# Cosine attention and low-rank mixer: the first batch's keys, its last pair's value products and its first mixer stage are arranged anew

## The chip, the cores and the metric

The kernel runs on one core of one Trainium2 chip. The metric is the device time of one execution in microseconds (us). The core has five engines, each with its own queue, which it works off in order: TensorE (PE in the profile, with its weight loads as PEld), VectorE (DVE), ScalarE (ACT), GpSimd (POOL) and SyncE (SP). GpSimd issues the loads of this kernel and SyncE most of the stores. Matmul results go to PSUM, which has eight banks of 512 float32 columns.

## The reference

For 8 batches, 12 heads, 448 tokens and 64 columns a head, queries and keys are normalised, their products divided by tau pass a softmax, and the values are averaged with it. The 12 heads side by side make x, 448 tokens by 768 columns. The mixer first adds a low-rank mix along the tokens (rank 32), and then a two-layer network along the columns, with 3072 hidden columns.

```
q_n = q / (norm(q) + 1e-6);  k_n = k / (norm(k) + 1e-6)
scores = q_n @ k_n.T / tau
attn = softmax(scores)
x = (attn @ v), heads side by side          # 448 x 768
u = x + (x.T @ U @ V).T                      # U: 448 x 32, V: 32 x 448
out = u + relu(u @ w_ch1) @ w_ch2            # 768 -> 3072 -> 768
```

## The kernel before, in words

**Tiles.** Heads are worked in pairs, six a batch. A token n is written as 4 s + c, with c from 0 to 3 and s from 0 to 111, so the 448 keys make four chunks of 112. `load_qk` brings the queries and keys of two or four heads, cast to bf16. `squares` and `scales` form the squares (ScalarE or VectorE, L538 and L540), their sums (L544), a logarithm and an exponential on ScalarE (L558, L559), and the inverse (L564, L566): the scale 1/(norm sqrt(tau)) of each row, kept in the tile `inv`.

**Normalised and raw keys.** `norm` multiplies queries and keys by their scales (L612, tile `xn`), transposes them on TensorE by a matmul with the identity (L468, through `flip`) and copies the result from PSUM to the tile `qkT` (L966 on ScalarE, L968 on VectorE). For the pairs listed in `RAW_KEYS` (L303: pairs 0 to 3 of batch 0) the keys aren't multiplied: they are transposed as loaded, and their scale comes in later, as the scale of the exponential, a number for each key row.

**Scores and exponentials.** `scores` forms, for a pair and a key chunk, the products of both heads into two banks (L670). A pair with normalised keys takes one exponential for both heads, 896 columns (L688). A pair with raw keys takes one for each head, 448 columns, since each head's keys have scales of their own (L683).

**Values.** `values` multiplies the exponentials by v, with a column of ones beside it which gives the softmax sum (L713): for each head four tiles t of 128 tokens, each summed over the four key chunks j. All four tiles of a head lie in one bank. All products of a head wait for all exponentials of the pair. Then VectorE takes the reciprocal of the sums (L720) and multiplies into X (L722, the array `muls` in order of heads).

**First mixer stage.** `stage0` projects X on U in three column parts, 0 to 511, 512 to 639 and 640 to 767 (L768), and copies each to A (L966, L968). For batch 0, `columns` then forms each of six column blocks of u, transposed: three matmuls of X with the identity (L744) and one of A with V (L749) add up in one bank, and one copy brings it to `uT` (L966). For the other batches u is formed by tokens (L815, L829) and transposed.

**Network.** `mlp` forms the hidden columns in 24 blocks f: six matmuls each over the column blocks of uT (L891), then relu on ScalarE or VectorE (L914, L916), then the second layer (L927) and the add of u (L938). In batch 0, the first three blocks f begin with column blocks 0 to 4, and take block 5 later.

**The order of the work** is set by a planner. Every instruction is an `Op` with an engine, an assumed duration, dependences, the buffers it takes and gives back, and a priority. TensorE's are put in streams; at each moment the planner takes the first stream (in the order in which they were made) whose next instruction is ready by its own reckoning. ScalarE's and VectorE's go by priority. PSUM banks are handed out by rings (`bank_ring`), which list the banks that a use may have and how many at a time. Before batch 0's network begins, gaps in TensorE's plan are filled with matmuls on a constant tile (L598, `warm_up`). What the planner finds becomes a fixed order on each engine; on the chip only the waits for data and buffers remain. In the kernel before, the streams of TensorE come in this order: fill, transposes, first batch's scores, values, first stage, scores of the others, network. The last part of the first stage and the last column block go in the stream of the values, and the banks of both come from `r_mm`.

Of the kernel before, what the change touches and what calls it, by code (L numbers as in the profile page):

```python
# [269 lines left out]
def kernel(  # L270
# [12 lines left out]
    nc = tc.nc  # L283

    B, H, S, D = q.shape
    C = H * D
# [15 lines left out]
    WIDE = 3  # L302
    RAW_KEYS = {(0, 0), (0, 1), (0, 2), (0, 3)}  # L303
    FILL = 0.7
# [71 lines left out]
    r_mm = bank_ring([(7,), (6,), (5,), (4,)], 3)  # L376
    r_av = bank_ring([(5,), (6,), (7,), (4,)], 2, (4, D + 8))
    r_sc = bank_ring([(0, 1), (2, 3), (4, 5)], 3)
    r_low = bank_ring([(5,), (4,), (3,), (2,), (1,), (0,)], 2)
# [29 lines left out]
    pe_tp = plan.stream("PE")  # L409
    pe_first = plan.stream("PE")  # L410
    pe_av = plan.stream("PE")
    pe_a = plan.stream("PE")
    pe_sc = plan.stream("PE")
# [241 lines left out]
    def scores(b, slots):  # L655
# [22 lines left out]
        for (p, c), sc in zip(slots, scs):  # L678
            _, _, (inv, a, scaled) = sets[p]
            attn, exps = attns[b, p]  # L680
            if (b, p) in RAW_KEYS:
                for hh in range(2):
                    exps.append(plan.add(Op("ACT", act_t(S, 0.08), lambda sc=sc, c=c, hh=hh, attn=attn, inv=inv, a=a: nc.scalar.activation(  # L683
                        out=attn.tile[0:SCH, c, hh, off:off + S], in_=sc.tile[0:SCH, hh, 0:S], func=AF.Exp,
                        scale=inv.tile[:, 1, a + hh, c:c + 1]), deps=[o, scaled], acq=[attn],
                        rel=[sc, inv], prio=0.1)))
                continue
            exps.append(plan.add(Op("ACT", act_t(2 * S, 0.08), lambda sc=sc, c=c, attn=attn: nc.scalar.activation(  # L688
                out=attn.tile[0:SCH if b < WIDE else 128, c, :, off:off + S],
                in_=sc.tile[0:SCH if b < WIDE else 128, :, 0:S], func=AF.Exp),  # L690
                deps=[o], acq=[attn], rel=[sc], prio=0.1 if b == 0 else 1)))

    def values(b, p, X):
# [9 lines left out]
        if b == 0 and p == 0:  # L703
            last_exp["first"] = [exps[0]]
        muls = []
        for hh in range(2):
            h = 2 * p + hh
            av, rd = Slot(r_av2 if BURST[b] > 2 else r_av, 1), Slot(r_rd, 1)
            for t in range(4):
                for j in range(SC):  # L710
                    first, last = t == 0 and j == 0, t == 3 and j == SC - 1
                    def fn(t=t, j=j, h=h, hh=hh, av=av):
                        nc.tensor.matmul(  # L713
                            out=av.tile[:, t, 0:D + 1],
                            lhsT=(attn if j < SC - 1 else even).tile[0:kp, j, hh, 128 * t:128 * (t + 1)],
                            rhs=v_t[b % 2][0:kp, h, j, 0:D + 1], start=(j == 0), stop=(j == SC - 1))
                    o = plan.add(Op("PE", 0.033, fn,
                        deps=exps + got[b, h, "v"] + attn_set + v_set[b] if first else (), acq=[av] if first else [],
                        rel=([attn] if even is attn else [attn, even]) if last else []), pe_av)
# [12 lines left out]
    prev = {}  # L732

    def columns(X, A, uT, muls, cc, a):

        c0 = 128 * cc
        mm = Slot(r_mm, 1)
        st = pe_a if cc < CC - 1 else pe_av
        X.uses += 1
# [3 lines left out]
        for t in range(3):  # L743
# [7 lines left out]
            start=False, stop=True, skip_group_check=True), deps=[a], rel=[A]), st)  # L751
        c = plan.add(Op("ACT/DVE", any_t(384), None, deps=[o], rel=[mm], prio=0))
        c.fn = lambda: copy_op(c, uT.tile[:, cc, 0:384], mm.tile[:, 0:384])
        return c

    def stage0(b, X, muls):
        par = b % 2
        bank = r_sc1 if b == 1 else r_low if BURST[b] > 2 else r_mm
        by_pe = b < PE_BATCHES
# [7 lines left out]
        def project(t, c0, c1, mm):  # L767
            nc.tensor.matmul(out=mm.tile[R * t:R * (t + 1), 0:c1 - c0], lhsT=U_sb[:, par, t, :],  # L768
                             rhs=X.tile[:, t, c0:c1], start=True, stop=True)

        def project_all():
            for (c0, c1), mm in zip(cols, mms):
                for t in range(4):
                    project(t, c0, c1, mm)
        if not by_pe:
            o = plan.add(Op("PE", 0.2 + 2 * pe_t(CH), project_all, deps=muls + consts[:2 + par], acq=mms + [A]), pe_a)
        for (c0, c1), mm in zip(cols, mms):
            need = [m for i, m in enumerate(muls) if i * D < c1]
            for t in range(4) if by_pe else ():
                o = plan.add(Op("PE", pe_t(c1 - c0) + 0.2 if t == 0 else 0.01,  # L780
                                lambda t=t, c0=c0, c1=c1, mm=mm: project(t, c0, c1, mm),
                    deps=need + consts[:2 + par] if t == 0 else (), acq=[mm, A] if t == 0 else [],
                    rel=[warm] if b == 0 and c0 == 0 and t == 3 else []),
                    pe_a if c1 < C else pe_av)
            a = Op("ACT/DVE", any_t(c1 - c0), None, deps=[o], rel=[mm], prio=0)
# [84 lines left out]
    def mlp(b, us, uT, ut):  # L870
# [18 lines left out]
        def up(f, mm, ccs):  # L889
            for cc in ccs:  # L890
                o = plan.add(Op("PE", pe_t(n), lambda cc=cc: nc.tensor.matmul(  # L891
                    out=mm.tile[:, 0:n], lhsT=w1_sb[:, cc, f * 128:(f + 1) * 128],
                    rhs=uT.tile[:, cc, 0:n], start=(cc == 0), stop=(cc == CC - 1)),
                    deps=([ut[cc], last_exp[0]] if b == 0 else ut if cc == 0 else []) + (
                        [w1_of[f]] if cc == 0 else []),
# [252 lines left out]
```

## Time and profile before

The median of three runs is 588.56 us (588.4 to 589.15). The profiled execution spans 586.5 us.

| what | us or share |
|---|---|
| TensorE busy | 578.0 us, 99% |
| VectorE busy | 301.7 us, 51% |
| ScalarE busy | 268.6 us, 46% |
| GpSimd busy | 89.8 us, 15% |
| first layer of the network, L891 | 233.2 us busy, 1152 matmuls |
| second layer, L927 | 231.3 us busy, 1368 matmuls |
| value products, L713 | 58.7 us busy, 1536 matmuls |
| scores, L670 | 53.3 us busy, 384 matmuls |
| exponentials, L688 and L683 | 137.8 us (161 instructions) and 17.4 us (32) |
| fill, L598 | 141 matmuls |
| chain that ended last | TensorE 94%, ScalarE 3%, VectorE 2% |

A row of a group gives the line of the kernel, the engine, the operation, the tiles, how many there are, the busy time and the mean duration of one. A row of the timeline gives the start, the time that the instructions of the row take together, and how many they are. Matmuls overlap, so their durations add up to more than the time that they take. A row of the stretches gives each engine's busy time between two moments.

### The profile page before, as it was taken

Reading aid. Unit: us, or ns where it says so; the run is one execution under the profiler, and the core shown is the slowest. Engines: PE = TensorE matmul, PEld = TensorE weight load, DVE = VectorE, ACT = ScalarE, POOL = GpSimd, SP = SyncE. Lnnn points to the kernel's source line nnn. Section 1 sums busy time; section 2 is a strip of 40 time slices with the busy share of each in tenths; the row PEclk is TensorE's granted clock in tenths of the full one; section 3 lists DMA queues with packets and bytes.
Section 4 is the critical chain, followed back from the end, with each engine's and each line's share of the span. In section 5 each row is a group of like instructions: output and inputs, shape, how many; then the busy total and the mean of one; then the engine's idle time right before and its main releaser. Section 6 shows DMA issues by size and latency. Waiting matters only on the chain.

```text
span 586.5 us, 11699 instructions
## 1 busy us (share of the span) xinstructions
PE 578.0 (99%) x4878; PEld 328.0 (56%) x4878; DVE 301.7 (51%) x725; ACT 268.6 (46%) x444; POOL 89.8 (15%) x128
## 2 busy tenths in 40 slices
PE   7999999999999999999999999999999999999997
PEld 5555656544556665555456655655446666654565
DVE  7869839999997677368514780254102241110011
ACT  7977743567443544444453445434454334024300
POOL 8234220142410050004000040000000000000000
PEclk9999999999999999999999999999999999999999
DMA  9999992799997486359355573331031100310021
GB/s 159 201 206 192 210 147 70 119 105 138 103 141 121 72 76 101 77 86 106 42 94 103 103 50 50 78 73 32 0 58 39 41 15 1 95 41 1 1 54 55
DMA packets 133332, 50.68 MB, mean 86 GB/s; under 512 B 98208, under 2 KB 133280, under 8 KB 133280
## 3 DMA queue, kind: packets, MB, share of 16 engines
q0 software_dynamic: 72160, 25.73, 38.6%
q1 hardware_dynamic: 61056, 24.19, 20.1%
q8 instruction: 38, 0.62, 0.4%
q14 instruction: 14, 0.11, 0.1%
q10 hardware_dynamic: 64, 0.02, 0.0%
HBM read 52.25 MB, written 11.01 MB: 108 GB/s over the span
## 4 chain that ended last, share of the span: by engine, by line
PE 94%; ACT 3%; DVE 2%; DMA 0%; issue 0%
PE bank L927 38%; PE bank L891 37%; PE bank L713 8%; PE bank L670 7%; ACT attn L683 2%; PE bank L815 2%; PE bank L468 1%; PE bank L768 1%; ACT sq L538 1%; DMA raw_uv<-in_q_dram 0%; DVE xn L612 0%; DVE ss L544 0%; DVE u_nat L829 0%; ACT qkT L966 0%; PE bank L749 0%
## 5 line engine op out<-in xcount | busy, mean ns | idle before, releaser
L891 PE MATMUL bank<-uT,w_sb 128*128 128x512 bf16 (+1 forms) x1152 | 233.2, 353 | 0.6 <-ACT uT L966 0.6
L927 PE MATMUL bank<-w_sb,relu 128*128 128x384 bf16 (+1 forms) x1368 | 231.3, 323 | 0.1
L688 ACT ACTIVATE attn<-bank 128x896 bf16<-128x896 f32 (+1 forms) x161 | 137.8, 922 | 112.4 <-PE bank L670 111.9
L927 PEld LDWEIGHTS <-relu 128*128 128x128 bf16 x1368 | 128.4, 98 | 90.4 <-issue 12.7
L891 PEld LDWEIGHTS <-w_sb 128*128 128x128 bf16 x1152 | 108.9, 98 | 102.9 <-issue 8.9
L914 ACT ACTIVATE relu<-bank 128x384 bf16<-128x384 f32 (+1 forms) x161 | 87.0, 541 | 142.6 <-PE bank L891 142.2
L938 DVE TENSOR_TENSOR O_sb<-bank,u_nat 128x384 f32<-128x384 f32 (+1 forms) x57 | 31.1, 548 | 184.4 <-PE bank L927 162.1
L544 DVE TENSOR_REDUCE ss<-sq 112x8 f32<-112x512 bf16 x96 | 62.6, 670 | 1.3 <-ACT sq L538 1.1
L713 PEld LDWEIGHTS <-attn 128*128 128x128 bf16 (+1 forms) x1536 | 55.7, 98 | 10.8 <-issue 3.3
L612 DVE TENSOR_TENSOR xn<-qk_nat,inv 112x512 bf16<-112x512 bf16 x91 | 58.9, 682 | 0.2
L713 PE MATMUL bank<-v_nat,attn 128*128 128x65 bf16 (+1 forms) x1536 | 58.7, 193 | 0.1
L670 PE MATMUL bank<-qkT 64*128 64x448 bf16 (+1 forms) x384 | 53.3, 357 | 1.4 <-ACT qkT L966 0.6
L490 POOL DMA_DIRECT2D qk_nat<-in_q_dram x24 | 17.5, 729 | 201.3 <-DVE xn L612 153.8
L720 DVE RECIPROCAL rd<-bank 128x4 f32<-128x4 f32 x96 | 16.7, 176 | 51.2 <-PE bank L713 50.8
L722 DVE TENSOR_TENSOR X_sb<-bank,rd 128x256 bf16<-128x256 f32 x96 | 40.1, 420 | 2.2
L540 DVE TENSOR_TENSOR sq<-qk_nat 112x512 bf16<-112x512 bf16 x89 | 34.1, 413 | 0.0
L670 PEld LDWEIGHTS <-qkT 64*128 64x128 bf16 (+1 forms) x384 | 13.2, 95 | 28.4 <-issue 24.3
L916 DVE TENSOR_SCALAR relu<-bank 128x512 bf16<-128x512 f32 (+1 forms) x31 | 19.8, 638 | 13.9 <-PE bank L891 13.7
L513 POOL DMA_DIRECT2D v_nat<-in_v_dram x30 | 22.1, 743 | 24.5 <-PE bank L713 24.5
L829 DVE TENSOR_TENSOR u_nat<-bank,X_sb 128x384 bf16<-128x384 f32 (+2 forms) x45 | 22.2, 524 | 5.4 <-PE bank L815 4.9
L490 POOL DMA_DIRECT2D qk_nat<-in_k_dram x24 | 16.8, 702 | 5.2 <-DMA w_sb<-in_moe_w_ch_dram 3.6
L683 ACT ACTIVATE attn<-bank,inv 112x448 bf16<-112x448 f32 x32 | 17.4, 654 | 0.0
(58 smaller groups left out, 182.7 us busy)
## 6 DMA issues: line engine op xcount, KB each, us to landing
qk_nat<-in_q_dram POOLq DMA_DIRECT2D x23, 224.0 KB, 5.0
qk_nat<-in_k_dram POOLq DMA_DIRECT2D x23, 224.0 KB, 5.9
w_sb<-in_moe_w_ch_dram POOLq DMA_DIRECT2D x4, 1152.0 KB, 21.3
w_sb<-in_moe_w_ch_dram POOLq DMA_DIRECT2D x8, 576.0 KB, 16.0
v_nat<-in_v_dram POOLq DMA_DIRECT2D x17, 168.0 KB, 8.9
out_dram<-O_sb SPq DMA_DIRECT2D x15, 168.0 KB, 2.2
out_dram<-O_sb SPq DMA_DIRECT2D x16, 144.0 KB, 2.1
out_dram<-O_sb SPq DMA_DIRECT2D x16, 120.0 KB, 2.0
```

The source lines that it names most:

```text
L490: ops = [load(lambda i=i, src=src: nc.gpsimd.dma_start(out=ld.tile[:, i, lo:lo + h1 - h0, :], in_=src[b, h0:h1].rearrange("h (s c) d -> s ...
L540: nc.vector.tensor_mul(y, x, x)
L544: lambda i=i, a0=a0, a1=a1, sq=sq: nc.vector.reduce_sum(ss.tile[:, i, a0:a1, :].rearrange("p h c -> p (h c)"), sq.tile[:, 0:a1 - a0, :].re ...
L612: nc.vector.tensor_mul(dst, src, sc)
L670: nc.tensor.matmul(out=out, lhsT=qkT.tile.rearrange("p b s -> p (b s)")[r, n0:n0 + w], rhs=qkT.tile[r, SC:2 * SC, :].rearrange("p c s -> p ...
L688: exps.append(plan.add(Op("ACT", act_t(2 * S, 0.08), lambda sc=sc, c=c, attn=attn: nc.scalar.activation(out=attn.tile[0:SCH if b < WIDE el ...
L713: nc.tensor.matmul(out=av.tile[:, t, 0:D + 1], lhsT=(attn if j < SC - 1 else even).tile[0:kp, j, hh, 128 * t:128 * (t + 1)], rhs=v_t[b % 2 ...
L722: muls.append(plan.add(Op("DVE", dve_t(256), lambda av=av, rd=rd, h=h: nc.vector.tensor_mul(X.tile[:, :, h * D:(h + 1) * D], av.tile[:, :, ...
L891: o = plan.add(Op("PE", pe_t(n), lambda cc=cc: nc.tensor.matmul(out=mm.tile[:, 0:n], lhsT=w1_sb[:, cc, f * 128:(f + 1) * 128], rhs=uT.tile ...
L914: nc.scalar.activation(out=relu.tile[:, f, 0:n], in_=mm.tile[:, 0:n], func=AF.Relu)
L927: nc.tensor.matmul(out=mm.tile[:, 0:c1 - c0], lhsT=relu.tile[:, f, i * 128:(i + 1) * 128], rhs=w2_t[:, f, c0:c1], start=(f == 0), stop=(f ...
L938: nc.vector.tensor_add(out=O.tile[:, 0:w], in0=mm.tile[:, 0:w], in1=us[i].tile[:, c0:c1]),
```

## The change

All of it concerns batch 0, in the first 42 us of the run. It has four parts.

1. `RAW_KEYS` holds pairs 0 and 1 alone. The keys of pairs 2 and 3 are normalised, and their exponentials take both heads at once. The planner's assumed duration of a 448-column exponential rises (0.08 becomes 0.143 in its fixed part).
2. In pair 5, the last of batch 0, the value products go by key chunk: those of chunk j, of both heads, depend on the exponentials of chunk j alone. The sums of the four token tiles of a head are thus open at once in one bank, and the start flag is set only on the first matmul of the bank. The products of batch 0 have bank rings of their own (`r_av0`, and `r_av5` for the last pair).
3. In batch 0, each of the three projections and each column block of the first stage gets a stream by its part: `pe_z0` for parts that need only the first heads, `pe_z1` for block 4, `pe_z2` for block 5, the last two ahead of the values. Their banks come from a ring over all eight (`r_z`). A projection is one `Op` of four matmuls that stay together, where before other work could come between.
4. The copy of the last column block to uT is split in halves of 192 columns, one on ScalarE and one on VectorE, with a priority ahead of the others.

Its purpose is to shorten the way from the first loads to the first network matmuls. The core of the diff:

```diff
-    RAW_KEYS = {(0, 0), (0, 1), (0, 2), (0, 3)}
+    RAW_KEYS = {(0, 0), (0, 1)}
...
+    r_av0 = bank_ring([(5,), (6,)], 2, (4, D + 8))
+    r_av5 = bank_ring([(5,), (6,), (0,), (1,), (2,), (3,)], 2, (4, D + 8))
+    r_z = bank_ring([(7,), (4,), (6,), (5,), (3,), (1,), (2,), (0,)], 4)
...
     pe_first = plan.stream("PE")
+    pe_z2 = plan.stream("PE")
+    pe_z1 = plan.stream("PE")
     pe_av = plan.stream("PE")
+    pe_z0 = plan.stream("PE")
     pe_a = plan.stream("PE")
...
-                    exps.append(plan.add(Op("ACT", act_t(S, 0.08), lambda sc=sc, c=c, hh=hh, attn=attn, inv=inv, a=a: nc.scalar.activation(
+                    exps.append(plan.add(Op("ACT", act_t(S, 0.143), lambda sc=sc, c=c, hh=hh, attn=attn, inv=inv, a=a: nc.scalar.activation(
...
+        ends = b == 0 and p == NPAIR - 1
+        ready = attn_set + v_set[b]
+        if ends:
+            for j in range(SC):
+                for hh, (av, rd) in enumerate(list(heads)):
+                    h = 2 * p + hh
+
+                    def fn(h=h, hh=hh, j=j, av=av):
+                        for t in range(4):
+                            product(h, hh, t, j, av, j == 0 and t == 0)
+                    o = plan.add(Op("PE", 4 * 0.033, fn, deps=[exps[j]] + got[b, h, "v"] + ready,
+                                    acq=[av] if j == 0 else [], rel=[attn] if j == SC - 1 else []), pe_av)
...
+    pe_z = [pe_z0] * (CC - 2) + [pe_z1, pe_z2]
...
-        mm = Slot(r_mm, 1)
-        st = pe_a if cc < CC - 1 else pe_av
+        mm = Slot(r_z, 1)
+        st = pe_z[cc]
...
-        c = plan.add(Op("ACT/DVE", any_t(384), None, deps=[o], rel=[mm], prio=0))
-        c.fn = lambda: copy_op(c, uT.tile[:, cc, 0:384], mm.tile[:, 0:384])
-        return c
+        cs = []
+        mm.uses = mm.left = 1 if cc < CC - 1 else 2
+        for n in range(mm.uses):
+            e, r = ("ACT/DVE", slice(0, 384)) if cc < CC - 1 else (("ACT", "DVE")[n], slice(192 * n, 192 * n + 192))
+            c = plan.add(Op(e, any_t(384 // mm.uses), None, deps=[o], rel=[mm], prio=0 if cc < CC - 1 else -1))
+            c.fn = lambda c=c, r=r: copy_op(c, uT.tile[:, cc, r], mm.tile[:, r])
+            cs.append(c)
+        return cs
...
-        bank = r_sc1 if b == 1 else r_low if BURST[b] > 2 else r_mm
+        bank = r_z if b == 0 else r_sc1 if b == 1 else r_low if BURST[b] > 2 else r_mm
...
+            if by_pe:
+                o = plan.add(Op("PE", 0.2 + pe_t(c1 - c0), lambda c0=c0, c1=c1, mm=mm: project_part(c0, c1, mm),
+                                deps=need + consts[:2 + par], acq=[mm, A],
+                                rel=[warm] if b == 0 and c0 == 0 else []),
+                             pe_z[c0 // 128] if b == 0 else pe_a if c1 < C else pe_av)
```

## The prediction

> **What bounds the kernel now.** I read the busy shares and the slices first, then the waits of TensorE, then the first 42 us engine by engine.
>
> ```profile
> PE 578.0 (99%) x4878; PEld 328.0 (56%) x4878; DVE 301.7 (51%) x725; ACT 268.6 (46%) x444; POOL 89.8 (15%) x128
> PE   7999999999999999999999999999999999999997
> ACT  7977743567443544444453445434454334024300
> ```
>
> TensorE is busy from end to end, so only work taken off it, or an earlier start of its real work, can shorten the run. The waits of TensorE after 41.8 us fill one line, and even that wait ends at 41.80:
>
> ```profile
> PE bank L891 <- ACT uT L966: 0.6, 1, 0.6
> ```
>
> So from 41.8 us TensorE runs a fixed amount of work without waiting. Before that, part of its busy time is filler (L598), and ScalarE is what is full:
>
> ```profile
> core 0: us, PE busy (x) PEld busy (x) DVE busy (x) ACT busy (x) POOL busy (x), PEclk, DMA share, GB/s
> 8.00:20.00 12.00, 10.15 (x127) 6.26 (x126) 10.80 (x26) 11.94 (x27) 6.63 (x9) 1.00 1.76 188
> 20.00:36.50 16.50, 15.87 (x222) 9.03 (x221) 11.60 (x36) 16.02 (x28) 5.32 (x7) 1.00 1.21 208
> 36.50:41.80 5.30, 4.71 (x65) 2.84 (x63) 4.61 (x13) 2.76 (x8) 2.16 (x3) 1.00 1.26 207
> 41.80:75.00 33.20, 33.20 (x318) 20.08 (x318) 28.22 (x67) 23.37 (x42) 10.50 (x14) 1.00 1.37 201
> ```
>
> The reader is to see 27.96 of 28.5 us of ScalarE busy from 8 to 36.5, and then a stretch of 5.3 us in which no engine but TensorE is full. Two rows of ScalarE's timeline give the price of its work:
>
> ```profile
> 21.57 8.48 ACT L683 ACTIVATE attn<-bank,inv 112x448 bf16<-112x448 f32 x16
> 29.83 6.67 ACT L688 ACTIVATE attn<-bank 112x896 bf16<-112x896 f32 x8
> ```
>
> The exponentials of a pair with raw keys are eight of 448 columns, since each head needs its own scale; those of other pairs are four of 896. From 21.57 to 29.83 are 16 of the first: 0.516 us each. Of the second, (6.67 - 0.92) / 7 = 0.821 us. A pair costs 4.13 or 3.28 us. After the last exponential (36.50) comes a chain that TensorE can't fill:
>
> ```profile
> 36.34 1.31 PE L713 MATMUL bank<-v_nat,attn 112*128 112x65 bf16 x32
> 37.94 0.42 DVE L722 TENSOR_TENSOR X_sb<-bank,rd 128x256 bf16<-128x256 f32 x1
> 38.75 0.33 PE L891 MATMUL bank<-uT,w_sb 128*128 128x384 bf16 x1
> 39.35 0.49 PE L891 MATMUL bank<-uT,w_sb 128*128 128x384 bf16 x2
> 40.20 0.23 PE L768 MATMUL bank<-X_sb,U_sb 128*32 128x128 bf16 x3
> 40.55 0.33 PE L891 MATMUL bank<-uT,w_sb 128*128 128x384 bf16 x1
> 40.90 0.34 PE L749 MATMUL bank<-V_sb,A_sb 128*128 128x384 bf16 x1
> ```
>
> In these 5.3 us only four first-layer matmuls (L891) get in.
>
> [...] Half as many instructions must save. [...] here 22 matmuls of L891 in 3.73 us are 0.163 us apart though their rows say 326 ns, so I count with distances. [...]
>
> **The change, part by part.**
>
> 1. *Keys of pairs 2 and 3 normalised.* ScalarE loses 2 x (4.13 - 3.28) = 1.7 us. VectorE gains two products of 0.60 us (L612: two in 1.27), 1.2 us. TensorE loses eight small transposes; nothing, since filler stands beside them. Added waiting: the scores of pair 2 now need its keys too. I follow VectorE in the new order. Its second reduction for heads 4 to 7 waits for a square on ScalarE that ends at 14.25, and ends at 14.97; the roots are on ScalarE till about 15.75, the inverse till 16.4, one more reduction to 17.0, two products to 18.25, a third to 18.85, two copies to 19.5. Scores then start near 20.0, behind pair 0's products, which need v (TensorE's first L713 is at 19.12). ScalarE gets there after eight exponentials of pair 1 and two squares, at 20.45, so the wait lies between 0 and 0.3. Pair 3 is ready at 22.2 and wanted at 24.1, pair 4 at 26.8 and 27.8, pair 5 at 28.8 and 31.1: VectorE stays ahead by 1 us or more.
>
> ScalarE's sum from 13.17, where both kernels have had the same sequence: before, 3 copies of 0.41, 3 squares of 0.52, 2 pairs of roots of 0.40, 24 x 0.516, 8 x 0.821, which is 22.5 and would end at 35.8 with the last one's tail of 0.1; it ended at 36.50, so 0.7 were waits. After: 2 copies, 4 squares, the same roots, 8 x 0.516 and 16 x 0.821, which is 21.0, ending at 34.2. With 0.3 for waits: last exponential at 34.55, 1.95 earlier. With none 34.25; with the old 0.7, 34.95.
>
> 2. *Last pair's products by key tile.* 32 products stood after the last exponential (36.34 to 37.65). Now 24 stand beside the exponentials and 8 are left: 8 x 0.033 + 0.16 for the last one's end, from 34.65 to 35.07. Both heads end together, so VectorE then does reciprocal, reciprocal, product, one column copy (it stands between in the new order) and product: 0.2 + 0.2 + 0.34 + 0.47 + 0.42 = 1.63, to 36.78. Before, the second head's product ended at 38.36, 1.86 after the last exponential; now 2.23. On this step alone nothing is won: the copy costs what the tile order saves.
>
> 3. *First stage by parts, streams and banks.* The gain is here: before, the last projection (L768) was pulled apart at 39.77 and 40.20 behind other parts, 1.84 us after its X was there, and its A copy stood behind two reductions on VectorE (40.55), so L749 came at 40.90 and uT at 41.75. After: projection at 36.88, three identity matmuls with it (0.35, as 39.00 to 39.35 before), four L891 matmuls (0.65) which hide the A copy on ScalarE (0.31), the last V product at 37.88, and from 38.05 a run of 39 first-layer matmuls. Nine of these need only the other columns: 9 x 0.163 = 1.47 us, which hide the last column's two half copies, even one after the other (0.3 each). By 38.05 six first-layer matmuls are done, before 41.80 four.
>
> Four of the five early columns (L744, L749) and the copies to uT lie on TensorE and ScalarE from 35.0 to 37.0, beside step 2's chain on VectorE: nothing. The half copy's wait on VectorE, with squares of the next batch ahead and normalisations behind it, costs nothing while those 1.47 us last. The planner's corrected price for L683 changes no instruction.
>
> *Sum.* 41.80 - 38.05 = 3.75, plus two more matmuls done, 0.33: 4.1 us. After it both orders hold the same matmuls of each shape, so 588.56 - 4.1 = **584.5**.
>
> Can the rest take it? Weights: the last chunk of the second layer is issued at 53.25 and takes 22.3 us, so it lands at 75.5; it is wanted after 63 second-layer matmuls that begin near 68, with others between near 83. The next-but-one batch's queries and keys land at 76.7 and 77.9 (56.33 + 20.4, 58.86 + 19.0) and VectorE reaches them near 82. Neither binds.
>
> **The rivals.**
>
> - *VectorE becomes the bound in the attention.* For: it is busy 11.60 of 16.5 and 10.80 of 12 us. Against: the margins of step 1. If the norms delayed ScalarE by all that it saves, the last exponential would stay near 36.5 and only steps 2 and 3 remain: 4.1 - 1.95, 2.1 us, 586.4.
> - *Gain given back at the next seam.* The second batch's transposes now stand behind 39 first-layer matmuls and begin near 44.4, before 45.38: one us earlier, where the first layer begins four earlier. Its last uT copy ended at 107.34, 1.76 us ahead of its first use at 109.10; by distances that use is now near 104.2, and the copy would end near 104.0. If it keeps only the 1 us, it ends at 106.3: TensorE waits 2.2 us, 586.7. Against: part of its chain was itself waiting for TensorE's turn.
> - *Slower.* VectorE is in order; a late load of the next-but-one batch ahead of the second batch's adds would stop it. It takes more than 5 us margin + 4 us gain: landing near 88 instead of 78 gives some 589.8. Only an upset DMA queue would do that, and the loads keep their order.
>
> **How the numbers follow.** Forecast 0.68, VectorE 0.13, seam 0.11, slower 0.05, no change 0.03. The low end takes no waits (0.3 better) and both columns' slack, 583.8; the high end takes the first two rivals in, 587.0. Faster: 0.68 + 0.13 + 0.11 and thus 0.92, which I cut to 0.89, for what an order with so many new places may hide; same 0.04, slower 0.07.
>
> **What would show it.** Right: last exponential at 34.3 to 35.0; 16 exponentials of 448 and 8 more of 896 than before; the long first-layer run from about 38; no TensorE wait over 0.5 us after it. Wrong: ScalarE idle before pair 2 or 4 and released by TensorE's scores; TensorE waiting for uT near 104 or for w_sb near 70 to 83.

## The result and the profile after

The changed kernel took 585.65 us in the median of four runs (585.09 to 586.07), the kernel before 588.86 in four runs beside it (588.4 to 589.32). The ratio is 0.9945, with a 95% interval of 0.9928 to 0.9962. A second measurement gave 585.84 against 588.53, ratio 0.9956 (0.9943 to 0.9968). So the change saves about 3 us, 3.2 in the first pair of medians and 2.7 in the second, where 4.1 were forecast. Lines of the code have moved: score matmuls are L676 (before L670), the exponentials L689 and L694 (L683, L688), the value products L717 (L713), their division L745 and L747 (L720, L722), projections L800 (L768), the columns' identity and V matmuls L771 and L776 (L744, L749), the copies L1001 and L1003 (L966, L968), the first layer L926 (L891), filler L604 (L598).

The profile shows one execution of each kernel. That of the changed kernel took 586.07 us, the longest of its four, and that of the kernel before 588.53; its spans therefore differ by 2.3 us (586.5 and 584.2) and not by 3.2. The page of the changed kernel, busy shares and slices:

```profile
PE 573.4 (98%) x4851; PEld 327.8 (56%) x4871; DVE 304.4 (52%) x731; ACT 265.8 (46%) x433; POOL 89.6 (15%) x128
ACT  7976643377623536343443455434454334024300
```

As before, only TensorE is full. A slice is 14.6 us long, and in the first three, where the change lies, ScalarE's digits are those of before; the slices are too coarse to show it. The stretches that the prediction had cut, in the changed kernel (columns: window, length, busy time of each engine with its instructions, granted clock, DMA share, GB/s):

```profile
20.00:36.50 16.50, 15.11 (x259) 10.31 (x258) 13.46 (x42) 15.24 (x22) 5.99 (x7) 1.00 1.21 208
36.50:41.80 5.30, 5.30 (x46) 3.30 (x44) 5.12 (x13) 2.91 (x8) 2.16 (x3) 1.00 1.27 206
```

From 36.5 to 41.8 TensorE is now busy for 5.30 of 5.30 us (before 4.71), and the work is real: the hole after the last exponential has closed. VectorE pays for it from 20 to 36.5: 13.46 us instead of 11.60. ScalarE's exponentials, two rows of its timeline:

```profile
16.22 3.77 ACT L689 ACTIVATE attn<-bank,inv 112x448 bf16<-112x448 f32 x7
28.70 6.71 ACT L694 ACTIVATE attn<-bank 112x896 bf16<-112x896 f32 x8
```

The last exponential ends at 28.70 + 6.71 = 35.41 (before 36.50). There are 16 of 448 columns and 16 of 896, where before there were 32 and 8. What TensorE does behind it:

```profile
28.95 1.02 PE L717 MATMUL bank<-v_nat,attn 112*128 112x65 bf16 x27
...
35.64 0.24 PE L800 MATMUL bank<-X_sb,U_sb 128*32 128x128 bf16 x4
35.82 0.34 PE L771 MATMUL bank<-ident,X_sb 128*128 128x128 bf16 x3
35.99 0.41 PE L717 MATMUL bank<-v_nat,attn 112*128 112x65 bf16 x8
...
38.14 0.24 PE L800 MATMUL bank<-X_sb,U_sb 128*32 128x128 bf16 x4
...
38.49 0.81 PE L926 MATMUL bank<-uT,w_sb 128*128 128x384 bf16 x4
39.14 0.33 PE L776 MATMUL bank<-V_sb,A_sb 128*128 128x384 bf16 x1
39.30 6.50 PE L926 MATMUL bank<-uT,w_sb 128*128 128x384 bf16 x39
```

The shape is the one that was forecast: last eight products, projection, four first-layer matmuls, last V product, and the run of 39. It begins at 39.30 (forecast 38.05), with six first-layer matmuls done ahead of it, as forecast. Before, with four done, it began at 41.80:

```profile
41.80 3.73 PE L891 MATMUL bank<-uT,w_sb 128*128 128x384 bf16 x22 [0.57 <-ACT uT L966]
```

Below, *tail* is the distance from the end of the last exponential to the start of the long first-layer run. Since kernels have different numbers of first-layer matmuls behind them by then, tails are also given "at four done": 0.163 us, the distance of two first-layer matmuls in these traces (39 of them take 6.50 us in the changed kernel, one alone 0.33), is taken off for each matmul above four and added for each below. Before: 5.30. Changed kernel: 3.89, and 3.89 - 2 x 0.163 = 3.56 at four done. Times from the start of the span are to be compared with care: the first exponential comes at 8.55 to 8.78 us in ten of the fourteen profiles, and at 9.23 or 9.34 in the other four, both profiles of the changed kernel among them.

### The profile page after: what moved, and what is told of

The parts are those of the page before. It is cut to its first block, busy times and chain, and to the rows that moved or that the text cites. A ratio compares the mean times of both kernels' runs of the same rounds, so it can differ in the third digit from the quotient of the medians.

```text
span 584.2 us, 11649 instructions
## 1 busy us (share of the span) xinstructions
PE 573.4 (98%) x4851; PEld 327.8 (56%) x4871; DVE 304.4 (52%) x731; ACT 265.8 (46%) x433; POOL 89.6 (15%) x128
## 4 chain that ended last, share of the span: by engine, by line
PE 94%; DVE 3%; ACT 1%; DMA 1%; issue 0%; DVEq 0%
PE bank L962 38%; PE bank L926 37%; PE bank L717 8%; PE bank L676 7%; PE bank L850 2%; PE bank L474 1%; DVE xn L618 1%; DVE ss L550 1%; PE bank L800 1%; ACT attn L689 1%; DMA raw_uv<-in_q_dram 1%; ACT sq L544 0%; DVE qkT L1003 0%; PE bank L771 0%; PE bank L896 0%
## 5 line engine op out<-in xcount | busy, mean ns | idle before, releaser
L926 PE MATMUL bank<-uT,w_sb 128*128 128x384 bf16 (+1 forms) x1133 | 228.8, 352 | 1.2 <-issue 0.3
L694 ACT ACTIVATE attn<-bank 128x896 bf16<-128x896 f32 (+1 forms) x169 | 144.0, 917 | 114.6 <-PE bank L676 114.5
L926 PEld LDWEIGHTS <-w_sb 128*128 128x128 bf16 x1152 | 109.5, 98 | 102.7 <-issue 7.2
L717 PEld LDWEIGHTS <-attn 128*128 128x128 bf16 (+1 forms) x1536 | 55.6, 98 | 9.5 <-issue 3.3
L618 DVE TENSOR_TENSOR xn<-qk_nat,inv 112x512 bf16<-112x512 bf16 x93 | 60.5, 682 | 0.2
L717 PE MATMUL bank<-v_nat,attn 128*128 128x65 bf16 (+1 forms) x1536 | 58.7, 193 | 0.3 <-DVE X_sb L747 0.2
L676 PE MATMUL bank<-qkT 64*128 64x448 bf16 (+1 forms) x384 | 51.1, 357 | 1.3 <-ACT attn L689 0.8
L745 DVE RECIPROCAL rd<-bank 128x4 f32<-128x4 f32 x96 | 16.9, 178 | 48.7 <-PE bank L717 48.4
L747 DVE TENSOR_TENSOR X_sb<-bank,rd 128x256 bf16<-128x256 f32 x96 | 40.0, 419 | 2.1
L676 PEld LDWEIGHTS <-qkT 64*128 64x128 bf16 (+1 forms) x384 | 13.0, 95 | 29.1 <-issue 25.2
L850 PE MATMUL bank<-A_sb,V_sb 128*128 128x384 bf16 (+2 forms) x62 | 14.4, 312 | 0.2 <-issue 0.2
```

The costliest lines, as they stand in the source:

```text
L618: nc.vector.tensor_mul(dst, src, sc)
L676: nc.tensor.matmul(out=out, lhsT=qkT.tile.rearrange("p b s -> p (b s)")[r, n0:n0 + w], rhs=qkT.tile[r, SC:2 * SC, :].rearrange("p c s -> p ...
L717: nc.tensor.matmul(out=av.tile[:, t, 0:D + 1], lhsT=(attn if j < SC - 1 else even).tile[0:kp, j, hh, 128 * t:128 * (t + 1)], rhs=v_t[b % 2 ...
L747: muls.append(plan.add(Op("DVE", dve_t(256), lambda av=av, rd=rd, h=h: nc.vector.tensor_mul(X.tile[:, :, h * D:(h + 1) * D], av.tile[:, :, ...
```

## The experiments

Of the kernels below, those of one group ran on one chip beside the kernel before. They are read by two numbers: the ratio of times, with its interval, and the tail in the profile.

### First group: which part brings how much

**The last two pairs' keys raw again, all else as in the changed kernel.**

```
-    RAW_KEYS = {(0, 0), (0, 1)}
+    RAW_KEYS = {(0, 0), (0, 1), (0, 2), (0, 3)}
```

> The changed kernel with the keys of four pairs raw again, as before; all else of the change stays. My theory (part 1 shortens ScalarE's exponentials by 1.95 us and the rest comes from the first stage): the last exponential ends about 1.7 to 2 us later than in the changed kernel, and the time is 1.5 to 2 us above it, some 587.4. Rival (VectorE's added products eat part of the gain by delaying the value path): under 1 us above the changed kernel, some 586.4. Rival (the keys are all of the gain): back at 588.9.

Measured: 587.01 us, ratio 0.9969 (0.9958 to 0.998). The last exponential ends at 36.89, no earlier than before. The tail is 3.04 us, 2.88 at four done: shorter than the changed kernel's. On TensorE, and on ScalarE:

```profile
32.70 0.28 PE L604 MATMUL bank<-warm 128*128 128x128 bf16 x2
...
39.93 1.30 PE L926 MATMUL bank<-uT,w_sb 128*128 128x384 bf16 x7
```

```profile
35.58 0.49 ACT L1001 CAST uT<-bank 128x384 bf16<-128x384 f32 x1
35.94 0.95 ACT L694 ACTIVATE attn<-bank 112x896 bf16<-112x896 f32 x1
```

TensorE still has room for filler at 32.70, as before (32.85). In the changed kernel the last filler stands at 27.36: from 28.95 on it works without a pause to the end of the attention. So parts 2 and 3 alone shorten the tail by 5.30 - 2.88 = 2.4 us, where I had forecast 2.1 for them. Some of this is only moved: a column copy of 0.49 us stands ahead of the last exponential here, where before all such copies came behind it. So a second count is needed, from the first exponential to the run, at four done: 33.13 us before, 30.54 here, 31.40 with part 1 alone (the next kernel), 29.74 in the changed kernel. By it parts 2 and 3 gain 2.6, part 1 gains 1.7, and both together 3.4 (3.6 in the second profile of the changed kernel). So 0.7 to 0.9 us of the sum is lost when part 1 is added. The times can't resolve so little: by the ratios it is 1.8 and 1.7 us alone against 2.6 to 3.2 together, each uncertain by 0.6 to 1.0.

**Part 1 alone on the kernel before**, with the planner's price for the exponential of 448 columns.

```
-    RAW_KEYS = {(0, 0), (0, 1), (0, 2), (0, 3)}
+    RAW_KEYS = {(0, 0), (0, 1)}
...
-                    exps.append(plan.add(Op("ACT", act_t(S, 0.08), lambda sc=sc, c=c, hh=hh, attn=attn, inv=inv, a=a: nc.scalar.activation(
+                    exps.append(plan.add(Op("ACT", act_t(S, 0.143), lambda sc=sc, c=c, hh=hh, attn=attn, inv=inv, a=a: nc.scalar.activation(
```

> The kernel before with the keys of two pairs raw and the new assumed cost of the 448-column exponential; nothing else of the change. My theory: the last exponential ends 1.7 to 2 us earlier than before, the time falls by 1.5 to 2 us to about 587.0. Rival (VectorE's products eat it): 588.0 or more. Rival (the keys are all of the gain): 585.7.

Measured: 586.85 us, ratio 0.9971 (0.9961 to 0.9981). Its ScalarE and its TensorE (the lines are those of the kernel before):

```profile
27.95 6.71 ACT L688 ACTIVATE attn<-bank 112x896 bf16<-112x896 f32 x8
```

```profile
39.97 3.73 PE L891 MATMUL bank<-uT,w_sb 128*128 128x384 bf16 x22 [0.57 <-ACT uT L966]
```

The exponentials end at 34.66, 1.84 us earlier, and the tail is 39.97 - 34.66 = 5.31, the old one to 0.01 us. The 1.84 us come through to the end: the median is 2.24 us below that of the kernel before (1.7 by the ratio). By these numbers part 1 does what step 1 says. The planner's new price is in this kernel too; what it does in the changed kernel is the last of these experiments.

**The changed kernel without the order by key tile.**

```
-        ends = b == 0 and p == NPAIR - 1
+        ends = False
```

> The changed kernel with the last pair's value products by token tile again, all of them after the pair's last exponential. My theory (tile order alone wins nothing, since both heads then end together and a column copy stands between): within 0.3 us of the changed kernel, 585.4 to 586.0. Rival (24 products of 0.032 us fewer behind the last exponential are on the path): 0.8 us slower, 586.4.

Measured: 585.95 us, ratio 0.9957 (0.9944 to 0.9969). Exponentials end at 34.51, the run begins at 38.17 with three matmuls done: a tail of 3.66, 3.82 at four done, 0.26 longer than with the order by key tile. The time can't be told from the changed kernel's.

**The changed kernel with the first stage in the old streams and banks**; its projection stays one operation.

```
-        mm = Slot(r_z, 1)
-        st = pe_z[cc]
+        mm = Slot(r_mm, 1)
+        st = pe_a if cc < CC - 1 else pe_av
...
-        bank = r_z if b == 0 else r_sc1 if b == 1 else r_low if BURST[b] > 2 else r_mm
+        bank = r_sc1 if b == 1 else r_low if BURST[b] > 2 else r_mm
...
-                              pe_z[c0 // 128] if b == 0 else pe_a if c1 < C else pe_av)
+                              pe_a if c1 < C else pe_av)
```

> The changed kernel with the first stage of the first batch in the streams and from the banks of before; each projection still one operation, the last copy still in halves. My theory (the first stage's own streams give about 2 us): about 2 us slower than the changed kernel, 587.6. Rival (the projection as one operation and the tile order gave that already): 586 or less.

Measured: 586.1 us, ratio 0.9953 (0.9939 to 0.9966). The profiled execution is the longest of five (588.05): it waited 0.8 us for a load of v, and its granted clock was 0.50 from 19.3 to 26.1 us. Both lie ahead of the last exponential, so only its tail is used: 41.24 - 36.92 = 4.32, with four done. That is 0.76 longer than the changed kernel's 3.56, and 0.98 shorter than before. I had put the whole gain of step 3 on streams and banks; a good half of it is there without them. The time does not even show the 0.76. One thing is better here than in the changed kernel:

```profile
37.18 0.41 PE L717 MATMUL bank<-v_nat,attn 112*128 112x65 bf16 x8
```

The last eight products begin 0.26 us after the last exponential, and in the changed kernel 35.99 - 35.41 = 0.58.

### Second group: step 3 taken apart

**The changed kernel again**, to stand beside the others.

> The changed kernel unchanged, on the chip of the runs beside it: the yardstick for them, and a second profile. It tells whether the late first exponential (9.23 us in the first profile of the changed kernel, 8.67 before) and the wait of 0.4 us near 87 us belong to the kernel. Theory: the start varies from execution to execution, so here the first exponential may be near 8.6 and the last near 34.6; the wait near 87 us stands. Rival: the start is late again. Time 585.6 to 585.9 on both.

Measured: 585.84 us, ratio 0.9956 (0.9943 to 0.9968); exponentials end at 35.17, the run begins at 39.07, six done: tail 3.90, as in the first profile (3.89). The first exponential is late again (9.23), so my theory of the start failed and its rival came true; the wait of 0.4 us near 87 us stands, as expected.

**Part 1 and only the streams and banks.**

```
+    r_z = bank_ring([(7,), (4,), (6,), (5,), (3,), (1,), (2,), (0,)], 4)
...
+    pe_z = [pe_z0] * (CC - 2) + [pe_z1, pe_z2]
...
-        mm = Slot(r_mm, 1)
-        st = pe_a if cc < CC - 1 else pe_av
+        mm = Slot(r_z, 1)
+        st = pe_z[cc]
...
-        bank = r_sc1 if b == 1 else r_low if BURST[b] > 2 else r_mm
+        bank = r_z if b == 0 else r_sc1 if b == 1 else r_low if BURST[b] > 2 else r_mm
...
-                    pe_a if c1 < C else pe_av)
+                    pe_z[c0 // 128] if b == 0 else pe_a if c1 < C else pe_av)
```

> The kernel before with part 1 and with the first stage's own streams and banks; its projections still four single operations, the value products by token tile, the last copy whole. Theory (streams and banks are what shortens the chain after the last exponential): the chain from the last exponential to the long first-layer run shrinks from 5.3 to about 4 us, time 1 us under part 1 alone, about 585.8, and the same as the changed kernel. Rival (tile order, single projection and half copies each carry a share): 586.4.

Measured: 586.19 us, ratio 0.996 (0.9947 to 0.9972). Exponentials end at 34.73, the run begins at 38.63 with three done: tail 3.90, 4.06 at four done. Against part 1 alone (5.31) the streams and banks bring 1.25 us.

**Part 1 and only the projection as one operation.**

```
-            for t in range(4) if by_pe else ():
-                o = plan.add(Op("PE", pe_t(c1 - c0) + 0.2 if t == 0 else 0.01,
...
+            if by_pe:
+                o = plan.add(Op("PE", 0.2 + pe_t(c1 - c0), lambda c0=c0, c1=c1, mm=mm: project_part(c0, c1, mm),
```

> The kernel before with part 1 and with each projection as one operation of four matmuls; streams, banks, products and copies as before. Theory (the split of the projection at the end was only a consequence of its stream): within 0.3 us of part 1 alone, about 586.7. Rival (keeping the four together is what freed the chain): 586.0 or less.

Measured: 586.64 us, ratio 0.9968 (0.9955 to 0.998). Tail 39.60 - 34.77 = 4.83, four done: 0.48 us less than part 1 alone. The two together would make 5.31 - 1.25 - 0.48 = 3.58 at four done if they added up, and the whole changed kernel has 3.56, with the order by key tile in it. So they overlap with the 0.26 of that order; all are of one chain. All this is read from tails: the times of this kernel, of the one before it and of part 1 alone can't be told apart.

**The last column copied whole by one engine.**

```
-        mm.uses = mm.left = 1 if cc < CC - 1 else 2
+        mm.uses = mm.left = 1
...
-            e, r = ("ACT/DVE", slice(0, 384)) if cc < CC - 1 else (("ACT", "DVE")[n], slice(192 * n, 192 * n + 192))
+            e, r = ("ACT/DVE", slice(0, 384))
```

> The changed kernel with the last column block copied whole, on one engine. Theory (the copy is hidden behind nine first-layer matmuls, 1.47 us): within 0.2 us of the changed kernel. Rival (the half copies are on the path): 0.3 us slower.

Measured: 585.86 us, ratio 0.9954 (0.994 to 0.9968); tail 38.38 - 34.49 = 3.89, six done, 3.56 at four. The halves bring nothing, as step 3 said: what they feed stands behind other first-layer matmuls.

### Third group: does more of the same help, and where is it given back?

**One raw pair instead of two.**

```
-    RAW_KEYS = {(0, 0), (0, 1)}
+    RAW_KEYS = {(0, 0)}
```

> The changed kernel with the keys of pair 1 normalised as well; only pair 0's stay raw. If ScalarE's exponentials were still the bound, the last one would end 4.13 - 3.28 = 0.85 us earlier and the time fall to about 585.0. Theory after the runs so far: VectorE has no slack left there, since two more of its products (0.6 us each) stand ahead of pair 1's scores; ScalarE waits for scores, and the time is not under the changed kernel's, 585.7 or more.

Measured: 593.71 us, ratio 1.0086 (1.0072 to 1.01): slower. The exponentials end at 35.68 and the run begins at 39.48 with six done: 0.2 us behind the changed kernel, so the loss of 8 us is not there. ScalarE does lose what fewer exponentials were to save: from the first (8.63) to the last they take 27.05 us, in the changed kernel 26.18. It waits 0.9 us for transposes and 0.5 us for scores, as the theory had it, and makes four of the copies to qkT instead of two. The large loss is later. Four windows of this kernel (columns as before):

```profile
104.00:108.00 4.00, 2.88 (x47) 1.69 (x44) 3.45 (x14) 2.21 (x4) 0.00 (x0) 1.00 0.10 29
108.00:112.00 4.00, 0.60 (x5) 0.40 (x5) 3.99 (x9) 1.40 (x2) 1.39 (x2) 0.83 0.53 88
112.00:116.00 4.00, 3.81 (x41) 2.52 (x41) 3.54 (x13) 2.07 (x4) 0.00 (x0) 0.50 1.39 140
116.00:120.00 4.00, 4.00 (x18) 1.43 (x17) 2.92 (x8) 1.79 (x3) 0.00 (x0) 0.82 0.54 83
```

From 108 to 112 TensorE (the first busy column) works 0.60 us of 4 while VectorE (the third) works 3.99, and the granted clock falls, to 0.50 in the next window. The longest wait of TensorE, and what VectorE does meanwhile:

```profile
112.19 1.42 PE L676 MATMUL bank<-qkT 64*128 64x448 bf16 x4 [2.41 <-DVE u_nat L861]
```

```profile
107.28 2.50 DVE L618 TENSOR_TENSOR xn<-qk_nat,inv 112x512 bf16<-112x512 bf16 x4
...
111.56 0.27 DVE L859 TENSOR_TENSOR u_nat<-bank,X_sb 64x128 bf16<-64x128 f32 x1
```

TensorE is done with L850, the matmul of A with V, at 109.78, but the adds that follow it (L859, L861) stand on VectorE behind four normalisations and the next squares and reductions. In the changed kernel the same adds of 128 columns run at 103.11 and 103.41, ahead of the normalisations at 109.81. Four score matmuls then take 1.42 us instead of 0.55.

VectorE's order is the last 1.8 us of the delay. The rest is older, for L850 itself ends 6.7 us later than in the changed kernel (103.09). It goes back to the second half of the scores of the second batch's last pair, in the changed kernel

```profile
91.59 0.55 PE L676 MATMUL bank<-qkT 64*128 64x448 bf16 x4
```

and here

```profile
100.34 0.55 PE L676 MATMUL bank<-qkT 64*128 64x448 bf16 x4
```

Before, they stood at 91.60. Their exponentials come at 100.75 instead of 92.00, the pair's products at 103.82 instead of 95.07, its projection at 106.31 instead of 100.52. TensorE had no listed wait ahead of these scores: it is their place in the planner's order that has changed. Why the planner moved them isn't shown.

**The changed kernel with another rule in the planner after 40 us**: an operation that would be ready within 0.08 us is waited for. Only the order of the later instructions changes.

```
-    HOLD = 0.0
+    HOLD = 0.08
...
-                            if r <= t + self.HOLD:
+                            if r <= t + (self.HOLD if t > 40.0 else 0.0):
```

> The changed kernel with a planner that, after its 40th us, keeps an engine free for 0.08 us when an operation ahead in priority is about to be ready. On VectorE this takes reductions and normalisations (0.6 us) out from between a reciprocal and its product, where the changed kernel has many. Theory (part of the earlier start is given back in waits for banks that VectorE frees late, 0.4 us near 87 us alone): this wait goes, and the time falls by 0.3 to 0.7 us to about 585.3. Rival (new waits come up elsewhere, whatever the order): 585.6 to 586.

Measured: 592.88 us, ratio 1.0066 (1.0053 to 1.0078): slower, in the same way; neither the theory nor its rival came true. The wait near 87 us is gone. The run begins at 39.66, but the same scores stand at 100.22 and the pair's products at 103.64. The adds (L859) come at 108.77, here behind squares and reductions, TensorE waits 1.98 us for them, and the clock falls:

```profile
108.00:112.00 4.00, 1.89 (x6) 0.55 (x6) 3.85 (x12) 0.88 (x3) 0.00 (x0) 0.67 0.41 113
112.00:116.00 4.00, 4.00 (x13) 1.32 (x13) 3.44 (x7) 2.10 (x3) 1.40 (x2) 0.50 0.59 78
```

**A third slot and two more banks for the products of the first batch's early pairs**, against the backlog on TensorE.

```
-    r_av0 = bank_ring([(5,), (6,)], 2, (4, D + 8))
+    r_av0 = bank_ring([(5,), (6,), (7,), (4,)], 3, (4, D + 8))
```

> The changed kernel with four banks to choose from and three at a time for the value products of pairs 0 to 4, where it has two banks. Theory: in the changed kernel pair 2's products (their exponentials end near 24.6) start only near 28.9, since VectorE frees pair 1's two banks late, behind the added normalisations; TensorE is then full till the end of the chain, and the last eight products come 0.4 us late. With a third bank they come earlier: the last eight products start within 0.25 us of the last exponential (0.6 in the changed kernel), time 0.2 to 0.4 us down, about 585.5. Rival (the backlog comes from TensorE's order, not from banks): no change, 585.8.

Measured: 585.6 us, ratio 0.9947 (0.9935 to 0.996), not to be told from the changed kernel. The exponentials end at 35.09, the last eight products begin at 35.65, and the tail is 3.87. The backlog stays: here too 26 products of a row begin only at 28.62. My guess that these banks were what delayed the products falls.

**The planner's old price for the exponential of 448 columns, in the changed kernel.**

```
-                    exps.append(plan.add(Op("ACT", act_t(S, 0.143), lambda sc=sc, c=c, hh=hh, attn=attn, inv=inv, a=a: nc.scalar.activation(
+                    exps.append(plan.add(Op("ACT", act_t(S, 0.08), lambda sc=sc, c=c, hh=hh, attn=attn, inv=inv, a=a: nc.scalar.activation(
```

> The changed kernel with the planner's old assumed duration of the 448-column exponential, 0.063 us too short. Theory (it changes no instruction, only places in the order): within 0.3 us of the changed kernel. Rival (the planner's wrong price was part of what made the kernel before slow): 0.5 us slower or more, over 586.3.

Measured: 586.57 us, ratio 0.9964 (0.995 to 0.9978). The tail is 3.85 and the run begins at 39.22, no later than in the changed kernel, but its first exponential is at 8.59 and not at 9.23. From the first to the last exponential it takes 26.78 us, 0.60 more than the changed kernel (26.18; 25.94 in its second profile). One row of ScalarE tells why:

```profile
19.66 1.97 ACT L1001 COPY qkT<-bank 128x448 bf16<-128x448 bf16 x4
```

Such a copy may go to ScalarE or VectorE, as the planner finds one free. With the low price ScalarE gets six of them between its first and last exponential, and three squares, where in the changed kernel it has two and four. So the price does change instructions: it changes who makes them. The median is some 0.7 to 0.9 us above the changed kernel's two medians, which fits, but the intervals overlap widely: for the time it is undecided.

## Why the prediction was right, and where its size was off

**Step 1, the keys.** Right. Part 1 alone ends the exponentials 1.84 us earlier (forecast 1.95, range 1.55 to 2.25), and VectorE stays ahead but for one place: the only listed wait of ScalarE for scores is 0.4 us (in the changed kernel at 27.47), and those scores stand on TensorE behind a transpose that waits 0.67 us for a copy on VectorE. A margin of "1 us or more" everywhere was too much. In the profile of the changed kernel the gain looks smaller, 36.50 - 35.41 = 1.09, and the last exponential lies outside the 34.3 to 35.0 that were named as the sign of being right. Its first exponential is at 9.23 instead of 8.67, so 0.56 is lost ahead of all exponentials, and the second profile starts at 9.23 too. But the kernel with the other planner rule, whose plan is the same for its first 40 us, starts at 8.70, and the whole-copy kernel has the same tail and starts at 8.60, yet its median is the same (585.86). So the late start is not shown to belong to the change, and its cause stays open. From the first exponential to the last are 27.83 us before and 26.18 after: 1.65 saved.

**Step 2, the order by key tile.** Right that it wins next to nothing: 0.26 us of tail, none that the times show.

**Step 3, the first stage.** Right in its mechanism, and here is the first term of the sum that was mis-sized: the tail was to be 38.05 - 34.55 = 3.5, and is 3.89. The failing term is "8 x 0.033 + 0.16 for the last one's end, from 34.65": the eight products were to start 0.1 us after the last exponential, and they start 35.99 - 35.41 = 0.58 after it. Some of these 0.48 us come back, because VectorE's five operations behind them, to the end of the last product (37.41 + 0.42 = 37.83), take 1.84 us from the products' start where I had 2.13; and 0.21 is lost again, since the projection comes 0.31 after that instead of 0.1. From there on it is as forecast: the last V product 1.00 us after the projection (39.14 - 38.14), the run 0.16 later. 0.48 - 0.29 + 0.21 = 0.40, which is the whole difference.

The products come late for two reasons, and the larger is part 3 itself. Directly ahead of them stand the projection and the identity matmuls of column block 4 (the rows at 35.64 and 35.82): 0.35 of the 0.48 us. They are there because block 4's stream comes ahead of the values. The forecast saw these columns "from 35.0 to 37.0, beside step 2's chain" and put them at nothing, without asking on which side of the last eight products they would fall. In the kernel with the old streams they don't stand there, and the products begin after 0.26 us; in the six other profiles with the new streams, the order by key tile and one or two raw pairs it is 0.49 to 0.59. Whether the time would fall if block 4 gave way is not shown: TensorE is full there (busy for 10.00 of the 10 us from 30 to 40), and what is moved has to go elsewhere.

The smaller part, at most 0.13, is that TensorE is behind. I had called the 24 other products hidden "beside the exponentials", which takes for granted that TensorE has room there. The profile of before had it, for filler stood there; afterwards 128 products, those of four pairs, stand between 28.95 and 36.40, with scores and projections between them and no filler. VectorE's timeline in the changed kernel:

```profile
24.54 1.89 DVE L618 TENSOR_TENSOR xn<-qk_nat,inv 112x512 bf16<-112x512 bf16 x3
...
28.49 0.41 DVE L747 TENSOR_TENSOR X_sb<-bank,rd 128x256 bf16<-128x256 f32 x1
```

Pair 1's products were done at 24.86 on TensorE, and VectorE, with the normalisations ahead, divided them only at 27.61 and 28.49; the next pair's products begin at 28.95, after both. That the added normalisations make the backlog agrees with the kernel that undoes part 1, which has filler up to 32.98. But with more banks the products came no earlier than 28.19, so it isn't the two banks alone; what else holds the products back is not shown.

The step also named a wrong owner within itself: "The gain is here" was meant for streams and banks. They bring 1.25 us alone, the projection as one operation 0.48 alone, and without the streams 0.98 of 1.74 us is there. The two half copies cost and bring nothing, as said; on the changed kernel's VectorE

```profile
39.85 0.36 DVE L1003 CAST uT<-bank 128x192 bf16<-128x192 f32 x1 [0.17 <-ACT uT L1001]
```

shows that the second half waits 0.17 us, and that the first, which ScalarE makes from 39.50 to 39.82, is what ends this wait. The halves of this bank were not copied side by side; why the second waits is not shown. That the planner's price "changes no instruction" is wrong: with the old one ScalarE makes six copies to qkT in this attention, with the new one two.

**The sum.** "After it both orders hold the same matmuls of each shape, so 588.56 - 4.1" is the second term that failed. In the profiled pair the run begins 2.50 us earlier with two more matmuls done (0.33), 2.83 in all, and the spans differ by 2.3: 0.5 us is given back later. The longest wait of TensorE behind the run is, in the list of waits of the changed kernel (total, times, longest):

```profile
PE bank L962 <- DVE X_sb L747: 0.4, 1, 0.4
```

The second layer's matmul at 87.50 waits for a bank that a division on VectorE frees (at 87.03), and a reduction of 0.66 us stands ahead of the division there. That is 0.36 of the 0.5. The second profile of the changed kernel has all its 4871 matmul records (the first lacks 20 of them) and the same wait, and no other that is listed behind the run; 3.06 us of earlier run leave 2.6 in the spans. But the wait can't be the whole reason: the whole-copy kernel has none behind its run and gives back as much (3.75 us earlier, spans 3.0 apart). What costs it there is not shown. In part 1 alone nothing of the kind is lost (0.03 us between the start of its run and its end). So of the forecast's 4.1 the profiled pair lacks 0.86 in the exponentials (0.56 of it at the start), 0.39 in the tail and 0.5 later: 1.75, which leaves 2.3. The medians, where the profiled execution is the longest of four, give 3.2 and 2.7; so 0.9 to 1.4 are missing. The tail and what is given back later, 0.9 together, can be laid to the kernel; the rest is within what its executions differ by. The times alone would not have told forecast from rivals: 585.65 and 585.84 lie inside the stated range, 583.8 to 587.0, but nearer to the 586.4 and 586.7 of the first two rivals than to 584.5. It is the traces that show the forecast's mechanism, some 1.2 us smaller than it was put.

**The rivals.** VectorE as the bound of the attention did not happen: the exponentials end earlier. No late load showed in the changed kernel. The seam of the second batch is not where it loses: the first matmul of 128x512 that needs the second batch's columns starts at 106.41, 2.7 us earlier than the 109.10 of before, and TensorE is busy for 3.95 of the 4 us around it. But the rival is real, and near. Two kernels which reach the long run within 0.4 us of the changed one end 7 us later, and lose most of it here, where the planner put the last pair's scores some 8.7 us later and VectorE's adds behind work for the next batch. With one raw pair TensorE idles 1.12 + 3.40 us from 104 to 112, and the low clock takes, by an estimate from the granted 0.50 and 0.82 of the windows above, 0.50 x 4 + 0.18 x 4 = 2.7 us from 112 to 120: 7.2 of the 7.4 by which its span is longer. The prediction took its margin at this seam (1.76 us) from the old order, and the order is what such an edit changes. It held here because the order came out well, which the forecast had no means to know: as far as this seam goes, that was luck.

## What to carry to other kernels

Where one engine bounds a stage and another a seam, price the two apart and look at whether the second engine keeps any slack (filler, idle time) once the first has been relieved: here ScalarE's 1.84 us came through whole while TensorE had filler to give up, and part of the next gain was lost when it had none. Where a planner makes the order, a small edit can move a few urgent operations by many microseconds, far from the edit: here four score matmuls by 8.7 us. Look up, in the new order, where each operation on the way to the next seams stands, and what stands ahead of it on its engine. And where a stream is put ahead of another, ask which of its operations will fall just before the one that the chain is waiting for.

## What was not expected of the hardware

The granted clock fell in three of the profiles, and no single wait that is seen ahead of a fall is longer than 1.9 us. In the kernel with one raw pair it was halved from about 110.6 to 117.4 us, in the one with the other planner rule from about 109.4 to 116.2 (estimates: worked out from 0.83 and 0.82, and from 0.67 and 0.98, in the windows above, with 1.00 and 0.50 taken as the only two levels). Ahead of the fall TensorE had waited 0.72, 0.82, 0.54 and, of a fourth wait, 0.9 us in the first, with work between, and 0.37 and 1.9 us in the second. The profiled execution of the kernel with the old streams has a third case, before and after 19.3 us:

```profile
15.90:19.30 3.40, 2.73 (x23) 1.18 (x22) 3.37 (x9) 3.40 (x7) 0.83 (x1) 1.00 1.77 184
19.30:26.10 6.80, 6.25 (x72) 4.21 (x71) 5.15 (x15) 5.14 (x9) 2.84 (x4) 0.50 1.18 212
```

Here TensorE was busy for 2.73 of the 3.40 us ahead of the fall, so it stood idle for 0.67 us there in all. The other four executions of this kernel have a mean clock of 0.999 or 1. The low clock lasted 6.8 us in each of these three cases, in the first two by the estimate. The kernel with the other planner rule has a fourth, shorter one, with TensorE busy for 9.94 of 10 us:

```profile
20.00:30.00 10.00, 9.94 (x143) 6.40 (x139) 8.77 (x27) 8.90 (x14) 3.18 (x4) 0.83 1.19 208
```

By the same estimate, 0.17 x 10 / 0.5, the low clock there makes about 3.4 us. What brings a fall, and what ends it, is not shown by these runs. In the second kernel, 10 matmuls of 128x512 that begin at 112.89, most of them at the low clock, took 3.94 us; 10 that begin at 117.25 took 2.33.
